# A fused recurrent-attention and feed-forward kernel on one core: its table of 2531 events in a new order

## The chip, the cores and the metric

The kernel runs on one core of a Trainium2 chip. The metric is device time in microseconds (us): the median over runs of the kernel, each run one execution of the whole program. The engines are TensorE (PE in the rows, with its weight loads as PEld), VectorE (DVE), ScalarE (ACT), GpSimd (POOL) and SyncE (SP), which here issues every DMA. Each engine executes its own instructions in the order in which they stand, and waits at semaphores for the others.

## The reference

For 32 heads (4 batches of 8), 768 steps and a head width of 48, a state matrix is carried from step to step and read before it is updated; then every token's 384 outputs go through a feed-forward layer with 2048 hidden units.

```python
k_n = k / (norm(k) + 1e-06)
for t in range(S):
    kt, vt, bt = (k_n[:, :, t], v[:, :, t], beta[:, :, t, None])
    y[:, :, t] = np.einsum('bhd,bhde->bhe', q[:, :, t], state)
    v_old = np.einsum('bhde,bhd->bhe', state, kt)
    state = state + bt[:, :, :, None] * np.einsum('bhd,bhe->bhde', kt, vt - v_old)
# x: y as (3072 tokens, 384)
h = x @ w_in
sp = np.maximum(h, 0.0) + np.log1p(np.exp(-np.abs(h)))
return (h * erf(sp)) @ w_out
```

## The kernel before

**The attention half** works on 12 chunks c of 64 steps. For each chunk the keys are loaded and squared (`load_step` L165, `norm_sq` L183 on ACT), summed and turned into step sizes (`norm_sum` L191 and `norm_ops` L202 to L215 on DVE), and their Gram matrices are made on PE (`gram_mm` L247 and L251) and scaled (`gram_d` L264, `gram_a` L258 on DVE). A triangular inverse follows. For chunks 0 and 1 it is done on DVE: `first_blocks` (L316, a transpose), 15 times `first_row` (L322 and L323), `first_back` (L327 and L329, two transposes), then small products on PE (`first_w` L340, `first_x` L351) with ACT and DVE copies of their results (`first_copy` L333, `first_w2` L344, `first_x2` L355). For later chunks POOL does it row by row (`solve_row` L363 and L364). Two halves are merged by `merge_t` (L391, DVE), `merge_e` (L400, PE), `merge_e2` (L405), `merge_z` (L413, PE), `merge_z2` (L417) and `merge_m` (L426, PE). Then 48 chain steps j, four per chunk, carry the state: `chain_u` (L461), `chain_s` (L474) and `chain_y` (L488) on PE, with DVE (`chain_u2` L467, `chain_s2` L482) or ACT between them.

**The feed-forward half** works on 12 groups g of 256 tokens. `x_tr` (L644, L645) transposes a group's outputs, two instructions per half; `x_all` (L523) spreads its maximum; `x_hi` (L661, ACT) and `x_lo` (L666, DVE) split it into two f16 parts. `ffn1` (L678) makes 16 blocks of the hidden layer, nine matmuls each; softplus (`e_sp` L704) and erf (`e_erf` L709) on ACT need different tables, and where the set changes, `table` puts an ACT_TABLE_LOAD in (L128). `h_out` (L691), `e_mul` (L713), `e_split` (L724, L722) and `e_rest` (L728) make two f16 parts of the product, and `ffn2` (L739 to L741), six matmuls per block, makes the output.

**The weights** arrive as 64-bit numbers and are made into f16 pairs in the kernel. `w_load` (L533) loads a twelfth of one matrix (512 KB); `w_mask` (L539, ACT), `w_low` (L543) and `w_bits` (L547, both DVE) rebuild a f32 from it. Four `w_sum` (L554, ACT) take the largest value of the matrix, `w_all` (L523, PE) spreads it, `w_scale` makes a scale of it, and for each of 16 blocks `w_hi`, `w_dif` (L603, L604: two f32 products and one f16 product on PE) and `w_lo` make the two parts. For `w_in` all this stands ahead of the first `ffn1`.

**The order.** Every call stands in a list of events with a due time. The list is sorted, and then a table of numbers, `ORDER`, puts it in the order in which the calls are made; that is the order of instructions on each engine. SP's queue is such an order too, and all loads and stores stand in it. 158 matmuls on a cleared tile (`warm`, `fill`, L143) compute nothing; they keep TensorE at work in the opening stretch.

```python
    ev.sort(key=lambda e: (e[0], e[1]))
    if ORDER:
        ev = [ev[i] for i in ORDER]
    ...
        for _, _, fn in ev:
            fn()
```

## Time and profile before

| what | before |
|---|---|
| median of 3 runs | 661.63 us (660.23 to 662.59) |
| the profiled execution's own time | 663.63 us |
| its span, first to last instruction | 661.9 us |
| granted TensorE clock, mean over the span | 0.986 |
| PE busy, PEld busy | 630.6 us (95%), 481.5 us (73%) |
| DVE, ACT, POOL busy | 468.8 us (71%), 468.6 us (71%), 357.7 us (54%) |

Busy time is the union of an engine's instructions. Matmuls are pipelined, so one that is given as 326 ns may stand 163 ns behind the one before it; distances between starts tell more of PE than durations. The profiled execution took 2.00 us more than the median.

### The profile page before, as it was taken

How to read it: one execution, taken by the hardware profiler on the slowest of the kernel's cores; microseconds unless marked ns; L12 is line 12 of the kernel's file. 1: busy time of each engine (PE TensorE's matmuls, PEld its weight loads, DVE VectorE, ACT ScalarE, POOL GpSimd, SP SyncE). 2: the span in 40 equal slices, each digit the busy share in tenths (PEclk: the TensorE clock that was granted, in tenths of full speed). 3: DMA queues.
4: the chain of work that ended last, by engine and by line, in shares of the span. 5: the costliest groups of instructions: out<-in, count | busy, mean ns of one | idle time of the engine just before them, and what ended most of it. 6: DMA issues, size and time to landing. Idle time of an engine off the chain costs nothing.

```text
span 661.9 us, 22889 instructions
## 1 busy us (share of the span) xinstructions
PE 630.6 (95%) x9866; PEld 481.5 (73%) x9866; DVE 468.8 (71%) x1032; ACT 468.6 (71%) x694; POOL 357.7 (54%) x524
## 2 busy tenths in 40 slices
PE   6788999999999999999899999999999999999996
PEld 4556668777768787777687677887776787777763
DVE  4977869878877886668766778875649765657541
ACT  2187898999768897656684677667566788768860
POOL 5081289779997259782489942239972321211322
PEclk8878999999999999999999999999999999999999
DMA  9875761673121740504622241531204210000102
GB/s 246 283 214 164 195 182 34 127 140 77 39 90 29 164 106 3 126 16 112 146 46 56 76 87 26 127 78 31 52 18 104 46 39 13 14 1 1 37 1 48
DMA packets 76421, 56.20 MB, mean 85 GB/s; under 512 B 57184, under 2 KB 66528, under 8 KB 76320
## 3 DMA queue, kind: packets, MB, share of 16 engines
q1 hardware_dynamic: 76320, 54.74, 33.9%
q8 instruction: 77, 1.26, 0.8%
q14 instruction: 24, 0.20, 0.1%
HBM read 42.14 MB, written 12.58 MB: 83 GB/s over the span
## 4 chain that ended last, share of the span: by engine, by line
PE 53%; DVE 16%; ACT 13%; POOL 7%; issue 5%; DMA 4%; SPq 1%; POOLq 0%; DVEq 0%; ACTq 0%
PE ph L678 17%; PE pr L739 7%; PE pr L741 6%; PE pr L740 6%; DVE H L713 3%; POOL xb L364 3%; ACT L128 3%; POOL tmp L363 2%; PE warm L143 2%; ACT L L709 2%; PE pc L488 2%; DVE H L691 2%; PE pm L426 1%; DVE z L467 1%; ACT L L704 1%
## 5 line engine op out<-in xcount | busy, mean ns | idle before, releaser
L678 PE MATMUL ph<-xh,w_in 128*128 128x256 f16 x1152 | 207.6, 273 | 2.7 <-ACT L L704 2.3
L678 PEld LDWEIGHTS <-w_in 128*128 128x128 f16 x1728 | 164.9, 98 | 30.2 <-issue 3.8
L128 ACT ACT_TABLE_LOAD x131 | 168.1, 1283 | 2.2
L728 POOL TENSOR_TENSOR L<-H,L 128x512 f16<-128x512 f32 x72 | 85.3, 1195 | 147.6 <-DVE L L724 96.7
L678 PE MATMUL ph<-xl,w_in 128*128 128x256 f16 x576 | 157.0, 273 | 0.0
L741 PE MATMUL pr<-w_out,L 128*128 128x384 f16 x384 | 125.2, 326 | 0.7 <-POOL L L728 0.7
L739 PE MATMUL pr<-w_out,L 128*128 128x384 f16 x384 | 125.4, 327 | 0.0
L740 PE MATMUL pr<-w_out,L 128*128 128x384 f16 x384 | 125.2, 326 | 0.0
L448 POOL TENSOR_TENSOR z<-v,nm 64x192 f32<-64x192 f32 x96 | 56.4, 587 | 104.6 <-DMA v<-vtok 59.8
L704 ACT ACTIVATE L<-ph,xct 128x512 f32<-128x512 f32 x96 | 65.7, 687 | 53.5 <-DVE H L691 48.5
L364 POOL TENSOR_TENSOR xb<-xb,tmp 128x31 f32<-128x31 f32 (+15 forms) x155 | 95.0, 613 | 12.2
L363 POOL TENSOR_TENSOR tmp<-gb,xb 128x31 f32<-128x31 f32 (+15 forms) x155 | 85.1, 549 | 27.0 <-DMA gb<-d 16.7
L713 DVE TENSOR_TENSOR H<-H,L 128x512 f32<-128x512 f32 x96 | 75.6, 795 | 27.9 <-ACT L L709 23.6
L691 DVE TENSOR_SCALAR H<-ph 128x512 f32<-128x512 f32 x72 | 49.2, 685 | 36.0 <-PE ph L678 27.5
L709 ACT ACTIVATE L<-L 128x512 f32<-128x512 f32 x96 | 58.6, 627 | 0.8
L741 PEld LDWEIGHTS <-L 128*128 128x128 f16 x384 | 37.6, 98 | 26.1 <-POOL L L728 1.4
L739 PEld LDWEIGHTS <-L 128*128 128x128 f16 x384 | 37.5, 98 | 21.8
L740 PEld LDWEIGHTS <-L 128*128 128x128 f16 x384 | 37.6, 98 | 20.8
L467 DVE TENSOR_TENSOR z<-pc,ga 64x192 f32<-64x192 f32 x80 | 28.4, 355 | 27.5 <-PE pc L461 26.0
L661 ACT ACTIVATE xh<-pt,xsx 64x128 f16<-64x128 f32 (+1 forms) x72 | 26.0, 395 | 24.6 <-PE pt L645 12.7
L143 PE MATMUL warm<-zero 128*128 128x384 f16 x158 | 35.0, 373 | 3.3 <-issue 2.2
L724 DVE CAST L<-H 128x512 f16<-128x512 f32 x72 | 35.7, 500 | 1.4
(157 smaller groups left out, 968.5 us busy)
## 6 DMA issues: line engine op xcount, KB each, us to landing
raw_in<-w_in SPq DMA_DIRECT2D x12, 512.0 KB, 8.0
raw_out<-w_out SPq DMA_DIRECT2D x12, 512.0 KB, 5.0
d<-A SPq DMA_DIRECT2D x20, 256.0 KB, 3.2
kpg<-kT SPq DMA_DIRECT2D x24, 192.0 KB, 4.5
k<-ktok SPq DMA_DIRECT2D x12, 384.0 KB, 4.6
v<-vtok SPq DMA_DIRECT2D x48, 96.0 KB, 2.7
qp<-qT SPq DMA_DIRECT2D x24, 192.0 KB, 3.5
out<-ob SPq DMA_DIRECT2D x48, 96.0 KB, 2.2
```

Of the source, the lines that this page charges most:

```text
L128: se.add_instruction(mybir.InstLoadActFuncSet(name=nc.get_next_instruction_name(), act_func_set_id=i, ins=[], outs=[]))
L363: ge.tensor_tensor(tv, G[:, s, s + 1:].unsqueeze(1).broadcast_to([P, ncol, nr]), Xv[:, :, s:s + 1].broadcast_to([P, ncol, nr]), op=ALU.mult)
L364: ge.tensor_tensor(Xv[:, :, s + 1:], Xv[:, :, s + 1:], tv, op=ALU.add)
L678: te.matmul(ph, w[:, i, kt * P:kt * P + P], G[x][:, :, ksl], start=(m == 0), stop=(m == 8))
L691: ve.tensor_scalar(dst, src, HSC, None, op0=ALU.mult)
L704: se.activation(unit("L", g, u), G["ph", u], AF.Softplus, bias=0.0, scale=G["ct"])
L709: se.activation(Lu, Lu, AF.Erf, bias=0.0, scale=1.0)
L713: ve.tensor_tensor(Hu, Hu, unit("L", g, u), op=ALU.mult)
L728: (ge if (g * NFF // EU + u) % GLM else ve).tensor_tensor(G["gl", u], unit("H", g, u), G["gh", u], op=ALU.subtract)
L739: te.matmul(G["po"][a], gh[:, o, asl], wout_h[:, i, :], start=(i == 0), stop=False)
L740: te.matmul(G["po"][a], gh[:, o, asl], wout_l[:, i, :], start=False, stop=False)
L741: te.matmul(G["po"][a], gl[:, o, asl], wout_h[:, i, :], start=False, stop=(i == NFF - 1))
```

## The change

`ORDER` is replaced by another permutation of the same 2531 events. All else in the file is the same.

```diff
-ORDER = (1,56,2,4,88,42,3,23,13,36,...)
+ORDER = (1,27,2,7,63,5,81,3,48,4,42,...)
```

Every engine executes the same instructions as before, with one exception: an ACT_TABLE_LOAD is made where softplus follows erf or erf softplus, and the new order has 139 such changes in place of 131. On PE the number of places where a f16 matmul is followed by a f32 one goes from 114 to 104.

**SP, the first loads.** `kpg` and `k` are the keys of a chunk in two layouts (the number behind the name is the chunk), `be` the step sizes, `raw_in` a twelfth of `w_in`, `v` values, `qp` queries. Before:

```order
L232 DMA kpg0_128<-kT 48x1024 x2
L165 DMA k0_133<-ktok 128x768
L533 DMA raw_in3_136<-w_in 128x1024
L165 DMA k1_139<-ktok 128x768
L232 DMA kpg1_141<-kT 48x1024 x2
L171 DMA be0_145<-btok 128x32
```

Now:

```order
L232 DMA kpg1_128<-kT 48x1024 x2
L165 DMA k1_132<-ktok 128x768
L165 DMA k0_135<-ktok 128x768
L232 DMA kpg0_138<-kT 48x1024 x2
L171 DMA be0_142<-btok 128x32
L533 DMA raw_in2_147<-w_in 128x1024
```

The load of a twelfth of `w_in` moved from between the two chunks' keys to behind them.

**DVE, the end of the first inverse.** L322 and L323 are its rows, L327 and L329 the transposes back. Before:

```order
L323 TENSOR_TENSOR w_out_101<-w_out_101 128x2x15
L543 TENSOR_SCALAR raw_in4_282<-raw_in4_282 128x512
L547 SCALAR_TENSOR_TENSOR w_in_100<-w_in_100,raw_in3_136 128x512
L327 STREAM_TRANSPOSE w_out_101<-w_out_101 128x32x32
L329 STREAM_TRANSPOSE w_out_101<-w_out_101 128x32x32
```

Now:

```order
L322 TENSOR_TENSOR w_out_101<-w_out_101 128x30
L323 TENSOR_TENSOR w_out_101<-w_out_101 128x2x15
L327 STREAM_TRANSPOSE w_out_101<-w_out_101 128x32x32
L543 TENSOR_SCALAR raw_in1_321<-raw_in1_321 128x512
L329 STREAM_TRANSPOSE w_out_101<-w_out_101 128x32x32
```

A `w_low` and a `w_bits` moved from ahead of the transposes to behind the first. Another such pair stood among the 15 rows and is gone from there, and one of the eight `gram_d` ahead of the first transpose (L316) now stands far behind it.

**ACT, the first instructions and those ahead of `first_w2` of chunk 0** (L344 on `pw0`). Before:

```order
L539 ACTIVATE w_in_100<-raw_in3_136 128x512
L183 ACTIVATE w_out_101<-k0_133 128x768
L183 ACTIVATE w_out_101<-k1_139 128x768
...
L344 COPY w_out_101<-pw1_508 128x256
L539 ACTIVATE w_in_100<-raw_in8_328 128x512
L333 COPY xm0_0_90<-w_out_101 32x16x32
L344 COPY w_out_101<-pw0_601 128x256
```

Now:

```order
L183 ACTIVATE w_out_101<-k1_132 128x768
L183 ACTIVATE w_out_101<-k0_135 128x768
...
L344 COPY w_out_101<-pw1_490 128x256
L273 COPY qp1_0_88<-pq1_0_361 64x512
L273 COPY qp1_1_89<-pq1_0_361 64x512
L539 ACTIVATE w_in_100<-raw_in3_182 128x512
L539 ACTIVATE w_in_100<-raw_in0_332 128x512
L539 ACTIVATE w_in_100<-raw_in2_147 128x512
L333 COPY xm1_1_93<-w_out_101 32x16x32
L344 COPY w_out_101<-pw0_584 128x256
```

The squares no longer stand behind a `w_mask`; between the two copies of `pw` there are now six instructions where there were two.

## Rows read from the trace of the kernel before

**Rows 1.** The page, busy time of each engine, its share of the span and instructions.

```profile
PE 630.6 (95%) x9866; PEld 481.5 (73%) x9866; DVE 468.8 (71%) x1032; ACT 468.6 (71%) x694; POOL 357.7 (54%) x524
```

**Rows 2.** Busy time by stretch: the stretch, its length, busy us and instructions of PE, PEld, DVE, ACT and POOL, the granted TensorE clock, DMA share and GB/s.

```profile
0.00:80.00 80.00, 65.37 (x1539) 43.88 (x1540) 59.60 (x149) 43.17 (x72) 29.75 (x42) 0.89 0.77 222
80.00:200.00 120.00, 117.68 (x1876) 90.61 (x1871) 95.83 (x209) 103.19 (x176) 100.37 (x146) 1.00 0.43 99
200.00:656.00 456.00, 447.26 (x6469) 347.03 (x6465) 312.80 (x674) 321.77 (x448) 227.57 (x337) 1.00 0.25 57
```

**Rows 3.** Groups of instructions by line, the matmuls that compute nothing: count, busy us, mean ns, idle time before them and what ended it.

```profile
L143 PE MATMUL warm<-zero 128*128 128x384 f16 x158 | 35.0, 373 | 3.3 <-issue 2.2 <-DVE zero L134 1.1
```

**Rows 4.** Who waited for whom on PE from 80 to 660 us: us in total, times, longest. There are 14 rows, which come to 9.7 us together; the first, one between and the last stand here.

```profile
PE ph L678 <- ACT L L704: 2.3, 4, 0.8
...
PE pc L488 <- DVE z L467: 0.5, 1, 0.5
...
PE pc L474 <- DVE z L467: 0.2, 1, 0.2
```

**Rows 5.** ACT in order of time from the start: start us, duration us, line, in square brackets the idle time ahead and what ended it.

```profile
7.92 0.66 ACT L539 ACTIVATE w_in<-raw_in 128x512 f32<-128x512 f32 x1 [5.90 <-DMA raw_in<-w_in]
8.48 0.83 ACT L183 ACTIVATE w_out<-k 128x768 f32<-128x768 f32 x1
9.63 0.84 ACT L183 ACTIVATE w_out<-k 128x768 f32<-128x768 f32 x1 [0.32 <-DMA k<-ktok]
```

**Rows 6.** The chain of work that ended last, 10 to 34 us, in order of time: start us, us, what.

```profile
10.63 0.87 DVE n L191
...
15.67 2.66 DVE w_out L264 x8
...
22.62 0.34 DVE raw_in L543
...
24.73 0.60 DVE w_in L547
...
29.90 0.32 DVE raw_in L543
30.22 0.60 DVE w_in L547
30.82 1.86 DVE w_out L327
...
32.81 1.25 PE pw L340 x82
```

**Rows 7.** The same chain, 36 to 75 us. "issue" is time in which PE waited for nothing that the profile shows.

```profile
36.14 2.44 issue
...
40.13 2.99 PE warm L143 x9
...
49.41 2.15 issue
51.56 3.66 PE warm L143 x13
...
57.22 0.58 ACT T L405
...
70.88 0.46 PE spin L523 x2
...
74.28 0.84 PE wd_in L603 x2
```

**Rows 8.** ACT in order of time, one row for each kind of instruction that the new order puts between 30 and 60 us: start us, duration us of the row, line, count.

```profile
26.73 1.19 ACT L273 COPY qp<-pq 64x512 f32<-64x512 f32 x2 [12.59 <-PE pq L251]
...
32.90 0.67 ACT L539 ACTIVATE w_in<-raw_in 128x512 f32<-128x512 f32 x1
...
42.54 0.60 ACT L333 COPY xm<-w_out 32x512 f32<-32x512 f32 x1
...
47.34 0.36 ACT L355 COPY xm<-pw 16x256 f32<-16x256 f32 x1
...
64.62 1.47 ACT L554 ACTIVATE raw_in<-w_in 128x1536 bf16<-128x1536 f32 x1
```

**Rows 9.** PE in order of time around 210 us, two f16 matmuls and the f32 product behind them: start us, duration us, line, count.

```profile
209.92 0.27 PE L678 MATMUL ph<-xl,w_in 128*128 128x256 f16 x1
210.03 0.27 PE L678 MATMUL ph<-xh,w_in 128*128 128x256 f16 x1
210.23 1.15 PE L251 MATMUL pg<-kpg 48*64 48x64 f32 x32
```

**Rows 10.** ACT and DVE in order of time from 128 us, the split of half a group's outputs: start us, duration us, line, count.

```profile
128.07 1.08 ACT L661 ACTIVATE xh<-pt,xsx 128x256 f16<-128x256 f32 x3
...
129.42 1.09 DVE L666 SCALAR_TENSOR_TENSOR xl<-pt,xsx,xh 128x256 f16<-128x256 f32 x3
```

**Rows 11.** Groups of instructions by line, the table loads: count, busy us, mean ns, idle time before them.

```profile
L128 ACT ACT_TABLE_LOAD x131 | 168.1, 1283 | 2.2
```

**Rows 12.** Busy time by stretch as in Rows 2, for 300 to 400 us.

```profile
300.00:350.00 50.00, 47.34 (x835) 38.00 (x833) 37.08 (x85) 34.59 (x49) 24.82 (x39) 1.00 0.44 101
350.00:400.00 50.00, 47.81 (x661) 36.15 (x658) 38.23 (x77) 31.71 (x45) 36.67 (x56) 1.00 0.31 72
```

More of the change, by code (lines that the diff above doesn't have):

```diff
@@ new lines @@
+ORDER = (1,27,2,7,63,5,81,3,48,4,42,6,450,12,65,13,32,49,9,77,58,37,43,52,66,14,68,64,73,57,44,78,360,82,11,85,8,98,105,102,101,10,93,108,19,17,202,89,254,109,183,18,208,238,118,146,121,228,124,15,128,23,132,24,135,25,26,139,28,29,142,30,31,147,33,34,151,35,38,154,39,40,158,41,45,46,47,163,188,50,51,53,166,153,162,170,231,54,184,59,60,61,62,67,70,71,270,75,76,88,91,229,288,177,36,20,56,79,241,80,284,84,191,86,185,87,90,92,227,95,96,273,130,99,161,205,243,21,74,249,114,221,55,100,212,104,106,94,107,251,299,110,112,194,219,305,149,449,312,72,22,223,215,451,198,206,113,16,115,210,116,117,120,122,256,123,125,217,127,313,129,131,134,247,197,316,200,456,234,322,235,199,136,137,140,169,144,141,97,143,145,148,126,150,152,297,464,155,138,156,159,160,164,260,165,472,168,236,172,173,176,174,245,175,179,171,180,181,182,237,186,187,280,189,192,267,252,459,222,445,193,1051,265,195,196,232,325,327,203,261,204,293,207,471,264,209,211,303,213,285,214,216,218,167,220,225,178,271,467,262,157,226,278,230,233,103,440,239,279,240,242,306,244,544,224,246,248,307,643,263,292,275,318,287,323,111,69,250,253,83,255,258,259,266,486,465,391,257,119,296,343,447,310,455,483,133,460,336,311,268,344,269,272,274,276,277,350,328,281,507,282,283,329,286,330,356,190,315,403,347,366,491,319,405,331,337,289,201,290,334,487,291,294,340,529,439,526,489,346,422,503,342,502,560,348,441,362,295,433,298,355,300,301,302,353,452,442,304,308,523,448,309,314,461,317,357,444,454,320,324,359,326,364,332,477,335,497,367,511,361,338,546,370,446,474,375,321,458,368,468,492,469,373,384,478,363,374,555,341,475,377,488,380,509,563,339,345,382,351,369,354,358,352,371,476,548,376,381,385,463,393,510,470,383,473,372,349,390,479,395,365,388,392,379,576,386,484,400,416,396,670,408,480,333,490,398,389,397,694,387,411,482,641,413,498,399,429,519,401,394,653,559,402,378,696,505,419,495,406,599,493,404,501,407,424,513,514,409,410,428,521,436,412,494,508,415,438,527,516,512,417,414,534,679,531,481,420,418,683,538,466,542,443,485,500,496,545,453,525,684,499,518,462,547,552,504,522,687,457,421,537,557,533,528,425,532,536,540,515,688,551,423,562,657,691,638,584,564,517,568,426,695,567,530,427,698,550,549,637,570,700,652,702,572,556,682,659,579,665,430,1049,541,721,585,553,664,654,431,535,588,646,561,587,714,590,741,520,432,434,697,598,565,616,524,701,577,606,722,435,596,703,613,554,578,593,506,724,731,569,621,597,437,769,748,539,573,603,625,711,566,580,737,582,629,604,543,574,558,571,586,755,632,575,623,581,639,644,611,602,583,601,592,666,607,594,628,612,677,610,655,615,743,589,752,618,620,681,732,758,600,624,635,765,622,689,671,633,848,650,645,707,720,685,706,728,626,883,649,692,746,730,693,595,690,712,757,709,723,717,719,745,605,784,627,713,735,1750,608,715,762,811,756,669,796,609,800,772,699,614,716,662,822,705,734,619,833,744,630,803,739,759,754,631,750,718,747,634,766,777,749,636,763,738,674,768,640,771,807,774,789,795,642,773,764,775,781,776,778,686,786,647,785,736,648,790,767,792,818,708,793,1069,710,783,651,805,798,799,656,865,797,831,658,726,804,829,660,873,661,813,801,837,810,832,812,663,780,742,842,845,948,725,782,877,704,913,787,727,897,729,838,1083,753,733,740,836,846,667,751,889,824,850,760,814,834,854,668,924,808,890,816,841,843,788,672,901,673,835,851,675,770,676,819,856,904,678,817,866,826,802,860,827,867,825,859,809,779,869,864,870,680,791,934,806,868,862,884,617,1073,815,847,794,878,839,905,844,876,849,852,1054,840,1089,853,882,914,830,857,855,886,875,828,861,858,872,879,917,863,871,921,885,874,922,918,880,898,887,881,908,892,888,896,972,946,895,900,1161,932,961,902,891,983,910,964,1064,894,920,820,953,931,911,899,956,927,903,906,985,909,916,761,959,937,923,943,997,929,993,1074,954,907,988,941,990,912,976,945,1077,968,915,984,1005,925,989,1078,919,970,1019,928,1081,926,1008,939,971,935,1014,952,1007,940,947,1047,955,950,1202,893,957,1053,962,930,933,1013,1037,1082,996,1021,958,1085,973,936,938,1087,1102,1086,1040,942,979,1084,1088,1031,951,960,1046,1110,1090,965,1092,1093,967,1095,978,1056,1131,1146,974,1097,1062,966,963,1059,1112,1132,821,949,1098,995,977,1018,1015,1028,1002,1068,969,980,1063,981,1138,1140,1034,1010,986,1071,944,1030,975,1066,1033,1311,982,1387,1035,1003,987,991,1039,994,1017,992,1042,1043,1122,1070,1048,1105,1120,1050,1121,1023,1113,1079,1124,1125,1139,1108,1020,1128,1107,1000,1029,1026,1136,1032,1094,1011,1142,1126,1012,1151,1228,999,1022,1221,1016,1080,998,1443,1027,1041,1100,1130,1096,1072,1111,1129,1103,1004,1001,1210,1076,1156,1382,1144,1145,1106,1178,1025,1044,1162,1232,1165,1038,1134,1239,1167,1147,1055,1172,1099,1101,1254,1057,1104,1149,1262,1058,1024,1247,1060,1150,1177,1241,1281,1157,1294,1422,1344,1179,1137,823,1159,1184,1160,1181,1045,1182,1250,1109,1168,1115,1197,1169,1257,1052,1175,1208,1176,1119,1061,1171,1153,1427,1217,1192,1135,1399,1276,1224,1188,1230,1258,1199,1200,1036,1148,1265,1234,1154,1185,1269,1267,1195,1240,1285,1183,1268,1190,1187,1067,1416,1244,1158,1320,1075,1201,1141,1206,1174,1114,1246,1118,1324,1272,1335,1273,1288,1327,1428,1209,1396,1248,1218,1164,1065,1198,1220,1297,1214,1203,1223,1091,1226,1252,1117,1227,1155,1204,1116,1225,1166,1291,1127,1173,1292,1123,1215,1133,1231,1259,1143,1211,1235,1194,1261,1152,1236,1264,1348,1287,1163,1242,1351,1293,1266,1205,1170,1243,1299,1270,1180,1189,1233,1186,1368,1275,1237,1309,1006,1278,1212,1207,1249,1339,1219,1316,1282,1216,1277,1289,1431,1346,1380,1432,1229,1298,1347,1315,1303,1352,1302,1295,1238,1318,1222,1325,1433,1245,1424,1283,1213,1435,1359,1274,1310,1256,1290,1314,1438,1436,1263,1280,1313,1524,1284,1271,1300,1286,1319,1371,1356,1251,1376,1384,1321,1379,1253,1381,1255,1363,1403,1373,1440,1451,1441,1437,1322,1406,1331,1329,1412,1418,1304,1360,1459,1308,1413,1388,1444,1353,1296,1455,1400,1307,1333,1420,1340,1334,1429,1336,1383,1326,1342,1496,1260,1393,1279,1497,1341,1395,1464,1462,1398,1330,1343,1454,2161,1306,1301,1332,1456,1401,1317,1305,1009,1323,1338,1473,1565,1405,1409,1350,1414,1312,1415,1328,1471,1354,1337,1365,1503,1370,1345,1355,1486,1458,1446,1469,1430,1193,1584,1408,1442,1453,1452,1196,1445,1450,1378,1488,1762,1507,1366,1474,1617,1489,1480,1374,1460,1625,1377,1375,1358,1349,1467,1514,1478,1492,1357,1466,1472,1477,1508,1386,1476,1461,1493,1407,1361,1541,1479,1463,1411,1485,1494,1501,1419,1490,1509,1505,1391,1520,1191,1392,1364,1394,1421,1484,1495,1423,1502,1522,1498,1523,1537,1519,1426,1385,1525,1531,1362,1512,1528,1534,1447,1511,1530,1546,1449,1545,1535,1434,1558,1468,1389,1465,1631,1517,1510,1470,1487,1555,1639,1390,1564,1540,1553,1513,1404,1475,1557,1542,1621,1547,1628,1570,1410,1560,1417,1640,1571,1569,1532,1580,1425,1538,1397,1539,1610,1515,1630,1657,1500,1636,1481,1550,1504,1806,1587,1518,1674,1561,1745,1660,1947,1562,1551,1439,1593,1683,1563,1596,1367,1604,1600,1597,1668,1572,1672,1603,1577,1613,1578,1612,1679,1607,1527,1448,1581,1521,1609,1483,1583,1457,1529,1536,1611,1482,1599,1615,1614,1568,1586,1591,1589,1698,1573,1616,1605,1759,1622,1491,1618,1606,1499,1624,1506,1627,1588,1632,1594,1787,1711,1516,1714,1629,1635,1526,1595,1633,1598,1602,1533,1567,1638,1543,1644,1682,1574,1734,1566,1685,1549,1654,1623,1696,1649,1641,1651,1655,1731,1620,1656,1646,1645,1544,1678,1369,1650,1652,1402,1637,1548,1785,1739,1662,1665,1661,1552,1659,1694,1666,1790,1663,1687,1673,1681,1579,1676,1658,1809,1719,1592,1653,1980,1791,1601,1576,1794,1684,1608,1690,1688,1619,1664,1707,1795,1781,1779,1796,1887,1693,1575,1722,1372,1582,1777,1697,1740,1692,1699,1626,1585,1689,1798,1703,1801,1783,1634,1792,1705,1744,1721,1706,1716,1695,1723,1643,1671,1763,1647,1746,1675,1712,1648,1701,1928,1709,1733,1717,1556,1748,1667,1704,1559,1756,1670,1827,1766,1758,1799,1849,1642,1677,1669,1761,1877,1702,1860,1834,1680,1710,1764,1715,1686,1718,1691,1765,1803,1836,1700,1729,1804,1743,1726,1817,1752,1768,1814,1769,1736,1793,1771,1737,1818,1800,1775,1747,1807,1816,1724,1708,2070,1727,1819,1822,1753,1772,1770,1757,1776,1713,1754,1778,1720,1773,1909,1821,1866,1826,1900,1824,2037,1782,1825,1920,1851,1728,1725,1738,1829,1742,1855,1933,1805,1870,1749,1784,1839,1810,1786,1856,1858,1812,1872,1788,1832,1808,1755,1835,1813,1865,1741,1823,1874,1868,1871,1861,1880,1815,1859,1881,1916,1890,1828,1892,1873,1882,1899,1894,1888,1875,1897,1751,1831,1876,1921,1833,1852,1878,1891,1994,1840,1893,1883,1554,1898,1837,1767,1885,1841,1931,591,1774,1843,1844,1886,1838,1842,1904,1903,1847,1780,1846,1930,1760,1789,1857,1864,1802,1905,1918,1848,1910,2003,1830,1811,1908,1923,1915,1820,1934,1884,1845,1926,1907,1973,1943,1911,1984,1853,1895,1950,1991,1956,1901,1902,1939,1967,1960,1732,1951,1927,1735,1935,1993,1932,1966,1797,1913,1976,1983,1970,1854,1924,1925,1590,1936,1914,1850,1940,1954,1944,1941,1946,1999,1972,1949,1862,1952,1869,2103,1958,1962,1988,1974,1995,2002,1968,1879,1998,1937,1978,1969,1889,1957,1896,1985,1961,1906,2013,2020,2000,1987,2014,1965,1863,1912,1990,2035,1867,1992,2007,2009,2042,2061,2072,2026,1929,2017,1959,1938,2074,1942,2082,2077,1996,2016,2019,1955,2025,1945,2023,2001,2065,2086,1948,2073,2078,1964,2004,2079,2008,2106,2041,2096,2015,1971,2024,2028,2029,2036,1982,2044,2039,2046,2051,2012,1989,2018,1997,2006,2021,2010,2085,2110,2047,1963,2005,2108,2045,2271,2151,2097,2048,2040,1977,1953,2059,2031,2162,1975,2057,1979,2094,1981,2060,2052,2294,2055,2062,2198,2056,2176,2022,2126,2027,2011,2221,2050,2120,2129,2030,2102,2066,2135,2058,2140,2068,2197,2145,2165,2084,2136,2107,2069,2087,2190,2032,2090,1730,2033,2123,2064,2169,1917,2075,2053,2043,2080,2092,2117,2081,2049,2034,1919,2038,2067,2054,1922,1986,2119,2105,2155,2063,2142,2148,2071,2113,2118,2122,2076,2124,2170,2083,2128,2132,0,2109,2131,2137,2111,2089,2138,2206,2166,2160,2164,2091,2217,2181,2178,2101,2099,2192,2104,2114,2219,2183,2115,2212,2172,2189,2220,2195,2334,2121,2100,2202,2226,2207,2236,2203,2242,2231,2223,2193,2232,2088,2216,2209,2130,2167,2225,2133,2215,2156,2228,2143,2224,2291,2158,2243,2116,2141,2229,2171,2144,2245,2146,2173,2196,2175,2248,2288,2253,2199,2258,2153,2180,2149,2201,2154,2095,2159,2208,2252,2240,2174,2177,2298,2250,2112,2204,2251,2302,2254,2187,2127,2303,2233,2300,2134,2179,2093,2257,2139,2185,2098,2188,2147,2235,2191,2307,2264,2152,2348,2274,2210,2269,2324,2260,2211,2255,2261,2265,2272,2292,2157,2297,2321,2277,2213,2266,2218,2182,2256,2230,2150,2262,2184,2168,2163,2263,2237,2268,2270,2280,2186,2286,2125,2273,2194,2275,2200,2312,2283,2304,2287,2205,2279,2289,2214,2317,2282,2222,2306,2227,2323,2259,2345,2247,2343,2313,2346,2351,2308,2336,2326,2318,2234,2328,2371,2366,2338,2239,2244,2361,2281,2342,2319,2284,2357,2325,2238,2293,2339,2241,2396,2359,2362,2340,2365,2383,2364,2295,2367,2393,2370,2347,2330,2375,2267,2381,2333,2349,2399,2309,2278,2374,2311,2285,2314,2315,2401,2403,2353,2290,2316,2320,2296,2377,2332,2422,2388,2378,2299,2327,2301,2390,2335,2412,2392,2322,2414,2305,2329,2415,2394,2417,2310,2382,2331,2395,2398,2408,2400,2337,2379,2419,2426,2404,2405,2384,2355,2409,2432,2385,2406,2352,2246,2341,2411,2421,2249,2356,2344,2424,2350,2369,2427,2354,2358,2360,2363,2441,2380,2368,2435,2372,2448,2443,2445,2425,2446,2276,2452,2449,2373,2451,2454,2429,2376,2485,2468,2387,2462,2475,2478,2386,2397,2389,2437,2391,2402,2439,2407,2487,2440,2455,2489,2410,2467,2423,2431,2505,2413,2479,2434,2416,2436,2420,2457,2418,2480,2458,2433,2430,2463,2438,2476,2442,2444,2477,2447,2502,2450,2459,2453,2428,2471,2461,2456,2464,2504,2460,2506,2490,2509,2465,2470,2469,2496,2473,2466,2472,2498,2510,2511,2492,2499,2474,2501,2482,2493,2481,2486,2513,2488,2516,2491,2518,2495,2483,2494,2507,2484,2497,2508,2519,2500,2512,2503,2514,2517,2515,2520,2521,2522,2523,2524,2525,2526,2529,2527,2528,2530)
```

1 line of the change is left out of this document (removed).

## The prediction

> **What bounds the kernel now.** I read the page first: PE is busy for 95% of the span and no other engine for more than 71% [rows 1]. Then busy time by stretch: the 95% hides two regimes [rows 2]. [...] Third, the waits on PE from 80 us on: 14 rows, 9.7 us together, none over 2.3 [rows 4]. So an order can gain little behind 80 us. What it can move is the point at which PE's useful work becomes dense.
>
> Last I read the chain ahead of that point. It runs through a load and ACT [rows 5], DVE from 10 to 32.8 us [rows 6], and then PE, with dummies and two stretches of "issue" in it, and ACT [rows 7]. It reaches the first block of `w_dif` at 74.28 us. I take that block as the milestone, since the new order puts exactly the same products ahead of it on PE, with 138 dummies ahead of it where there were 140. What comes behind it on PE is therefore the same work too, and if the milestone comes X earlier and nothing new is waited for behind it, the end comes X earlier.
>
> **Term 1, the first loads: -2.2 us.** Before, a `w_mask` stood first on ACT, so the first square started at 8.48 us, behind a weight load; the second waited for its key load until 9.63 [rows 5], and the sum behind it started at 10.63 [rows 6]. The weight load came in by 7.92 and the 384 KB of keys behind it by 9.63: 1.7 us. The 512 KB of weights at that rate take 2.3 us, so the first keys were there by about 5.6. Now the two key loads follow each other ahead of all weights: the second is there by about 7.4 (estimate from those three times), its square of 0.84 ends at 8.3, and the sum can start at 8.4, 2.2 us earlier. Bounds: 0, if the second load is as late as now, and -2.6, if it is there at 7.0.
>
> **Term 2, DVE's first inverse: -2.2 us.** Out of DVE's unbroken run between that sum and L327 go two `w_low` (0.34 + 0.32), two `w_bits` (0.60 + 0.60) and one of eight `gram_d` (2.66 / 8 = 0.33) [rows 6]: 2.2 us. They come back behind it, where ACT sets the pace (term 3). L327 then starts at 30.82 - 4.4 = 26.4.
>
> **Term 3, from the inverse to the milestone: -5.6 us more.** L327, a `w_low` and L329 end at about 26.4 + 1.86 + 0.32 + 1.9 = 30.5. `first_w` of chunk 1 takes 1.25 behind L327 [rows 6], so its copy ends at 29.9. Then ACT has six instructions: a pair L273 (1.19), three masks (0.67 each), one L333 (0.60) [rows 8], 3.8 us, and the other copy ends at 34.1. To the end of the second `merge_e2` of chunk 0 it then has 8 masks (5.4), 2 squares (1.7), 6 L333 (3.6), 3 L355 (1.1), a pair L273 (1.2) and the two L405 (1.2): 14.2 us, to 48.3. Before, that point was 57.22 + 0.58 = 57.8 [rows 7]. Why 9.5 us earlier and not 4.4: before, PE stood 2.44 us in "issue", and had 9 dummies for 2.99 us and 13 for 3.66 on the chain [rows 7]; now ACT's own work fills those stretches, and PE's dummies lie beside it. That goes on: `merge_z` (1.2 on PE), a pair L417 (1.2), 1.0 for the last copies, a table load (1.28) [rows 11], four `w_sum` (1.6 each) [rows 8], a mask and a pair L405 (1.9) come to 13.0, so 61.3; from `w_all` to `w_dif` it was 74.28 - 70.88 = 3.4 [rows 7], of which 0.6 is a `chain_u` that now stands earlier. That makes 64.1, or -10.2 us. I take **-10** for terms 1 to 3 together, because PE has little to spare there: between the two `merge_z` are 25 dummies and some 5.6 us of products in 9.7 us. [...] Bounds: -4.4 (only terms 1 and 2 survive) and -12.
>
> **Term 4, behind the milestone on PE: +1.** A f32 product behind a f16 matmul starts 0.20 us after it, another f16 one 0.11 [rows 9]. With 104 such places in place of 114 that gives -0.9. Against it stand tighter places. Counted in PE work by the order, at 9 x 0.11 = 0.98 us per `ffn1` block, four groups now have 1.90, 2.08, 2.08 and 2.45 us between their last `x_tr` and the first `ffn1` that reads it; before, none had under 2.52. The split between takes 1.08 on ACT and then 1.09 on DVE, of which three parts overlap a little [rows 10]; with 2.5 as the need the shortfalls come to 1.5. And a `chain_y` stands only 1.0 us behind its `chain_u` six times, where it was three; the one such wait in the trace took 0.5 [rows 4]. Together about +2, so +1 net. Bounds: -1 and +6, if every tight place waits twice its shortfall.
>
> **Term 5, ACT's table loads: 0.** Eight more, at 1283 ns each [rows 11], are 10.3 us of ACT. They lie around the fourth and fifth group (11 more there, 2 fewer in the first), where ACT idles 100 - 66.3 = 33.7 us of 100 [rows 12]. That idle time hides them; if it were gone, they would cost 10.3. The rows show 2.2 us of idle time ahead of all 131 together [rows 11]. [...]
>
> **Term 6, the other waits behind the milestone: 0**, since they were 9.7 us [rows 4] and the new ones can't be read from the order. Bounds: -6 and +8.
>
> Sum: 663.63 - 10 + 1 = 654.6 for an execution like the profiled one, which took 2.0 us more than the median. So **652.6** for the median.
>
> **The rivals.**
> - *The opening gains as said, and the waits shrink too* (0.22). For it: between a `chain_u` and its `chain_s` the new order has a median of 5.2 us of PE work, before 4.5. Against: 9.7 us [rows 4] is all there is. With -12 and -6: 663.6 - 12 - 6 - 2 = 643.6.
> [...]
> - *The head start is eaten* (0.08): ACT is busy for 103.19 of 120 us between 80 and 200 [rows 2] and sets the pace there, so PE arrives early and waits. Against it: ACT's work ahead of that stretch is no more than before, and it idled 36.8 of the first 80 us [rows 2]. 663.6 + 1 - 2 = 662.6.
> - *Slower, by the table loads* (0.08). The place is the fourth and fifth group: 11 more loads are 14.1 us of ACT, and L704 must read one of two `ph` buffers before PE can fill it again. L704 already heads PE's waits [rows 4]. If the loads bunch where a buffer is due, up to 14.1 us reach PE: 652.6 + 14.1 = 666.7. It decides from the point where over 11 of the 14.1 us land on PE; 33.7 idle us speak against that. [...]
>
> **How the numbers follow.** A measurement of this kernel can tell 0.3%, 2 us, from no change: faster means under 659.6, slower over 663.6. My forecast has 0.47. Its own range is 648 to 657. Faster: 0.47 + 0.22 + 0.12 of the third case = 0.81. Same: the rest of the third, 0.03, and 0.06 of the head start eaten = 0.09. Slower: the rest, 0.10. From 641 to 662 the range leaves out a third of the first rival and the slower cases, some 2 in 10.
>
> **What would show it.** Right: the second L191 starts near 8.4 us, L327 near 26, the second L405 of chunk 0 ends near 48, the first `w_dif` starts near 64, and from there to PE's last matmul it takes as long as before, within 3 us. ACT_TABLE_LOAD stands at x139 with PE's waits on L704 no longer than now. Wrong: the milestone comes after 70, with "issue" or dummies at 0.33 us on the chain ahead of it; or it comes early and PE's waits from there on come to over 15 us; or the fourth and fifth group take longer than before.

## The result, and the profile after

The new order is slower: 667.26 us (median of 20 runs, 663.86 to 672.47) against 662.89 us of the order before (20 runs on the same chip), a ratio of 1.0065 with a 95% interval of 1.0044 to 1.0086. The prediction was 652.6 us and faster. The profiled execution of the new order took 672.47 us, the longest of the 20, so below I lean on medians and on what several traces share, not on the length of one.

The page and the stretches, which answer to [rows 1, 2, 11]:

```profile
span 670.7 us, 22870 instructions
PE 636.6 (95%) x9866; PEld 486.3 (73%) x9866; DVE 473.4 (71%) x1032; ACT 480.3 (72%) x702; POOL 357.2 (53%) x524
L128 ACT ACT_TABLE_LOAD x139 | 178.3, 1283 | 2.4
```

```profile
0.00:80.00 80.00, 68.57 (x1557) 47.50 (x1559) 61.64 (x148) 42.64 (x72) 28.94 (x42) 0.96 0.75 223
80.00:200.00 120.00, 116.53 (x1873) 90.34 (x1870) 98.59 (x212) 102.31 (x175) 100.89 (x146) 1.00 0.42 97
200.00:656.00 456.00, 441.93 (x6388) 342.92 (x6387) 311.72 (x672) 333.75 (x455) 225.49 (x336) 0.99 0.26 58
```

Behind 200 us PE now idles 456 - 441.93 = 14.1 us where it idled 8.7, and the granted clock is 0.99 in place of 1.00. The table loads are 139, as forecast.

**The opening.** DVE in order of time (start, duration, what), and the chain of work that ended last, 10 to 75 us (start, us, what), which answers to [rows 6, 7]:

```profile
9.00 0.95 DVE L191 TENSOR_REDUCE n<-w_out 128x16 f32<-128x768 f32 x1 [1.56 <-ACT w_out L183]
...
27.93 1.97 DVE L327 STREAM_TRANSPOSE w_out<-w_out 128x1024 f32<-128x1024 f32 x1
```

```profile
12.17 1.52 issue
...
21.91 6.26 PE warm L143 x21
...
34.38 2.39 issue
...
43.38 3.69 issue
...
48.09 6.27 PE warm L143 x28
54.36 1.13 PE pe L400 x64
...
73.70 0.84 PE wd_in L603 x2
```

The inverse is ready 2.8 us earlier, but from 10 us on the chain runs through PE alone: its products, its dummies (27.7 us of the chain) and "issue" (8.6 us). By its own row the first `w_dif` starts at 73.6 us; it was 74.2.

**Behind it.** PE's largest waits from 80 us on, which answer to [rows 4] (who for whom: us, times, longest):

```profile
PE sp L523 <- DVE xm L624: 2.8, 4, 1.0
PE ph L678 <- ACT L L704: 2.1, 4, 0.9
PE pm L426 <- DVE xl L666: 2.1, 1, 2.1
PE pr L741 <- POOL L L728: 1.8, 3, 1.1
PE pz L413 <- ACT T L405: 1.5, 1, 1.5
PE pc L474 <- DVE z L467: 1.4, 2, 1.1
```

PE in order of time around 228 us (in brackets the idle time ahead and what ended it):

```profile
227.74 1.20 PE L413 MATMUL pz<-xm,T 32*32 32x32 f32 x64 [1.50 <-ACT T L405]
229.93 0.79 PE L523 MATMUL sp<-ident,xm 128*128 128x128 f32 x2 [0.99 <-DVE xm L624]
230.52 0.53 PE L739 MATMUL pr<-w_out,L 128*128 128x384 f16 x1
230.84 0.53 PE L740 MATMUL pr<-w_out,L 128*128 128x384 f16 x1
...
235.82 0.33 PE L741 MATMUL pr<-w_out,L 128*128 128x384 f16 x1
235.98 0.27 PE L644 MATMUL pt<-ident,y 128*128 128x128 f32 x1
```

Behind two waits of 1.5 and 0.99 us, 15 matmuls stand 0.32 us apart in place of 0.16, at a granted clock of 0.50 from 231 to 235.5 us: 2.4 us more. The waits themselves start on other queues. The first starts on DVE. L413 needs both halves of a copy L405; ACT's half waited 3.42 us for DVE's, and that stood behind an `e_mul` (L713) of 1.77 us:

```profile
223.99 1.77 DVE L713 TENSOR_TENSOR H<-H,L 128x512 f32<-128x512 f32 x1
...
226.39 0.68 DVE L405 COPY T<-pe 32x512 f32<-32x512 f32 x1
```

The median of the 96 L713 is 0.68 us; this one ran beside POOL's L728 (224.06 to 225.21), of which the last section has more. Eight traces have the new rest without a mending at this place. In seven the L713 there took 1.77 to 2.00 us and L413 waited 1.5 to 1.7 us; in the eighth (`after_half_dummies`) no L713 there was over 1.2, and L413 did not wait over 1 us.

The second wait starts on SP. SP, then DVE, in order of time:

```profile
218.40 0.46 SPq L369 DMA_DIRECT2D d<-xb  x1
221.36 1.92 SPq L384 DMA_DIRECT2D xm<-d  x4
223.38 2.52 SPq L289 DMA_DIRECT2D d<-A  x2
```

```profile
228.40 0.69 DVE L258 TENSOR_TENSOR A<-pg,gn 128x512 f32<-128x512 f32 x1 [1.33 <-DMA d<-A]
```

`to_dram` (L289) stands on SP behind `from_blocks2` (L384) of chunk 5, which waits for the store of `put_blocks` (L369) and is not needed before 248 us. So the store of A is late, `gram_a` (L258) waits to overwrite A, and all that is behind it on DVE, the maximum L624 among it, waits too; PE's 0.99 us are for L624.

A second such place is at 520 us. DVE and SP in order of time, then two `ffn1` pairs from the chain, 512 to 546 us:

```profile
523.85 0.62 DVE L747 TENSOR_SCALAR ob<-pr,xco 128x384 f32<-128x384 f32 x1 [2.99 <-DMA out<-ob]
```

```profile
520.61 0.35 SPq L441 DMA_DIRECT2D v<-vtok  x1
521.05 4.55 SPq L755 DMA_DIRECT2D out<-ob  x6
```

```profile
532.31 3.63 PE ph L678 x18
...
537.12 2.08 PE ph L678 x18
```

A store of output stands on SP behind loads of `v` that wait for POOL; DVE needs its buffer and waits 2.99 us; PE waits 0.84 us for L624 and 2.1 for L666 behind it, and then 18 matmuls take 3.63 us instead of 2.08, at a granted clock of 0.50 from 532.7 to 535.9 us (1.00 from 536.1 to 540). A third place, at 410 us, costs PE 2.2 us (waits for L728 on POOL and L704 on ACT).

### The profile page after: what moved, and what is told of

It reads as the page before. It is cut to its first block, busy times and chain, and to the rows that moved or that the text cites. A ratio compares the mean times of both kernels' runs of the same rounds, so it can differ in the third digit from the quotient of the medians.

```text
span 670.7 us, 22870 instructions
## 1 busy us (share of the span) xinstructions
PE 636.6 (95%) x9866; PEld 486.3 (73%) x9866; DVE 473.4 (71%) x1032; ACT 480.3 (72%) x702; POOL 357.2 (53%) x524
## 3 DMA queue, kind: packets, MB, share of 16 engines
q8 instruction: 77, 1.26, 0.8%
## 4 chain that ended last, share of the span: by engine, by line
PE 53%; DVE 16%; ACT 10%; POOL 10%; issue 5%; DMA 5%; SPq 1%; POOLq 0%; DVEq 0%; ACTq 0%
PE ph L678 15%; PE pr L739 6%; PE pr L741 6%; PE pr L740 6%; PE warm L143 4%; POOL xb L364 4%; POOL tmp L363 3%; ACT L128 3%; DVE H L713 2%; PE pc L488 2%; POOL L L728 2%; PE pc L461 2%; PE pq L251 2%; DVE H L691 2%; DMA d<-A 2%
## 5 line engine op out<-in xcount | busy, mean ns | idle before, releaser
L728 POOL TENSOR_TENSOR L<-H,L 128x512 f16<-128x512 f32 x72 | 85.4, 1197 | 163.7 <-DVE L L724 123.9
L704 ACT ACTIVATE L<-ph,xct 128x512 f32<-128x512 f32 x96 | 65.5, 687 | 56.4 <-DVE H L691 50.3
L448 POOL TENSOR_TENSOR z<-v,nm 64x192 f32<-64x192 f32 x96 | 53.6, 558 | 92.9 <-DMA v<-vtok 59.0
L363 POOL TENSOR_TENSOR tmp<-gb,xb 128x31 f32<-128x31 f32 (+15 forms) x155 | 87.5, 565 | 24.4 <-DMA gb<-d 14.4
L713 DVE TENSOR_TENSOR H<-H,L 128x512 f32<-128x512 f32 x96 | 73.5, 774 | 27.5 <-ACT L L709 14.6
L724 DVE CAST L<-H 128x512 f16<-128x512 f32 x72 | 41.0, 577 | 1.3
L666 DVE SCALAR_TENSOR_TENSOR xl<-pt,xsx,xh 64x128 f16<-64x128 f32 (+1 forms) x72 | 25.8, 386 | 15.5 <-ACT xh L661 15.0
```

Of the source, the lines that this page charges most:

```text
L363: ge.tensor_tensor(tv, G[:, s, s + 1:].unsqueeze(1).broadcast_to([P, ncol, nr]), Xv[:, :, s:s + 1].broadcast_to([P, ncol, nr]), op=ALU.mult)
L704: se.activation(unit("L", g, u), G["ph", u], AF.Softplus, bias=0.0, scale=G["ct"])
L713: ve.tensor_tensor(Hu, Hu, unit("L", g, u), op=ALU.mult)
L728: (ge if (g * NFF // EU + u) % GLM else ve).tensor_tensor(G["gl", u], unit("H", g, u), G["gh", u], op=ALU.subtract)
```

## The experiments

Medians of all kernels that were timed more than once (6 to 20 runs), with the ratio to the order before, measured beside it on the same chip. Where I compare two of these kernels with each other and their intervals overlap, the difference is not clear of noise.

| kernel | us | ratio, 95% interval |
|---|---|---|
| the new order | 667.26 | 1.0065, 1.0044 to 1.0086 |
| open_before_rest_after | 678.16 | 1.0231, 1.0206 to 1.0255 |
| open_after_rest_before | 664.86 | 1.0033, 1.0006 to 1.0059 |
| seam_before_after | 672.07 | 1.0130, 1.0082 to 1.0178 |
| seam_after_before | 661.05 | 0.9964, 0.9940 to 0.9989 |
| after_half_dummies | 664.65 | 1.0028, 1.0004 to 1.0052 |
| after_no_dummies | 665.90 | 1.0051, 1.0028 to 1.0075 |
| before_half_dummies | 664.87 | 1.0029, 1.0005 to 1.0054 |
| repair_220 | 670.75 | 1.0110, 1.0069 to 1.0151 |
| repair_220b | 665.38 | 1.0030, 1.0007 to 1.0052 |
| repair_520 | 664.42 | 1.0016, 0.9994 to 1.0038 |
| repair_all | 666.05 | 1.0048, 1.0023 to 1.0073 |
| repair_all_half | 667.47 | 1.0052, 1.0021 to 1.0082 |
| repair_three | 662.82 | 0.9994, 0.9970 to 1.0017 |

**Half of one order, half of the other, cut at the first `w_dif`.** The edit, in both directions:

```diff
-ORDER = new
+ORDER = p + [i for i in other if i not in p]   # p: one order up to w_dif("in", 0)
```

> All events up to the first w_dif of w_in stand as in the order before, all later ones as in the new order. Theory (the loss stands behind the opening: waits of DVE and PE in the new order from 200 us on, and TensorE's clock that falls behind two of them; the opening itself came out even): the first w_dif starts at 74.3 us as before, the time is some 668 us, ratio to before 1.005 to 1.010, and PE loses 5 to 10 us between 200 and 560 us as in the new order's profile. Rival A (the new opening hands on late work, and that is what costs later): with the old opening the later part loses nothing, 663 us, ratio 0.998 to 1.002.

> The reverse: the new order up to the first w_dif of w_in, the order before from there on. Theory (the loss stands behind the opening): the first w_dif starts at 73.6 us, and from there it takes as long as before: 662 us, ratio 0.997 to 1.001. Rival A (the new opening hands on late work): ratio 1.004 to 1.009, about 667 us.

Neither came out as expected by either theory. The cut itself cost time: from the first `w_dif` to the first `ffn2` it took 59.4 us (old opening, new rest) and 61.5 us (the reverse) where the two whole orders take 54.5 and 54.1. PE there waited 4.1 and 3.4 us for L611 on ACT; 15 events of the old opening and 9 of the new one stand on the other side of the cut in the other order. But the loss behind 200 us was there with the old opening as well. That called for a better cut.

**The same at a seam** where both orders have made the same events but for four (event 555, some 110 us):

> The new order for its first 555 events (to about 110 us), the order before for the rest; at that point the two have done the same events but for four. Theory (the opening gained some 3 us: six executions with the new opening whole reached the first ffn2 at 122.4 to 127.7 us, mean 125.3, the one of before at 128.7; the rest loses some 8): the gain stays and the loss is gone, 658 to 661 us, ratio 0.993 to 0.998. Rival A (the opening is worth nothing in the end): 662 to 664 us. Rival B (the seam costs what it did at the first w_dif): 664 us or more.

> The reverse: the order before for its first 555 events, the new order for the rest. Theory: the loss of the rest without the gain of the opening, 668 to 672 us, ratio 1.008 to 1.014, with PE idle for 3, 2 and 3 us in 200 to 240, 400 to 440 and 520 to 560. Rival A (the new opening hands on late work to the rest): 662 to 664 us.

The theory holds in both, each median less than 0.1 us beyond its range: the new opening with the old rest takes 661.05 us and beats both orders; the reverse takes 672.07. The opening's gain is smaller with the old rest (1.5 us by the medians) than with the new one (672.07 - 667.26 = 4.8). PE in three stretches (length, then busy us of PE, PEld, DVE, ACT, POOL, clock, DMA), the first kernel and then the second:

```profile
200.00:240.00 40.00, 39.91 (x710) 33.42 (x706) 35.53 (x85) 34.39 (x45) 18.27 (x32) 1.00 0.55 121
400.00:440.00 40.00, 39.37 (x661) 31.68 (x657) 30.49 (x73) 28.55 (x41) 7.67 (x13) 1.00 0.40 87
520.00:560.00 40.00, 39.69 (x612) 31.74 (x613) 23.96 (x51) 34.99 (x46) 7.32 (x9) 1.00 0.09 22
```

```profile
200.00:240.00 40.00, 36.99 (x603) 29.24 (x602) 32.95 (x72) 31.21 (x43) 22.12 (x35) 0.96 0.39 77
400.00:440.00 40.00, 37.90 (x536) 28.54 (x535) 30.66 (x73) 27.28 (x40) 11.05 (x15) 1.00 0.42 97
520.00:560.00 40.00, 37.34 (x694) 29.94 (x689) 26.71 (x61) 25.50 (x37) 6.41 (x8) 0.96 0.15 35
```

In the four traces with the old rest PE idles at most 0.8 us in each of these and the clock is 1.00 in all. In the thirteen with the new rest, mended or not, it idles up to 5.8 us in one, and in each of them the clock is below 1.00 in one to three of the three stretches. Where it falls differs from run to run (in 200 to 240 us from 0.91 to 1.00).

**Fewer dummies.**

```diff
-ORDER = new
+ORDER = [i for i in new if i not in dropped]   # dropped: every second, or all 130, fill() ahead of w_dif("in", 0)
```

> The new order with every second of the 130 dummies ahead of the first w_dif left out (they compute nothing). Theory (PE's dummies set the pace of the new opening: PE waits for no engine between 13.7 and 70 us, and 130 dummies take some 30 us there): 65 dummies less are up to 14 us less on PE, until ACT's chain sets the pace near 64 us; the first w_dif starts at 64 to 68 us and the time falls by 5 to 9 us against the new order, to 658 to 662 us, ratio to before 0.993 to 0.999. Rival C (PE's instructions can't come faster, so that the dummies only fill time that would stand in 'issue'): the first w_dif starts at 72 us or later, 'issue' on the chain grows from 8.6 us to over 15, and the time stays at 667 us.

> The new order with all 130 dummies ahead of the first w_dif left out. Theory (PE's dummies set the pace of the new opening): PE waits for ACT and DVE again; the first w_dif starts near 64 us, as worked out in the prediction for the chain of ACT. [...] Rival C (PE's instructions can't come faster): first w_dif at 72 us or later, with over 20 us of 'issue' ahead of it, and 667 us or more.

> The order before with every second of its 140 dummies ahead of the first w_dif left out (66 less). If PE's dummies hold up that opening too (in its chain 9 took 2.99 and 13 took 3.66 us), the first w_dif comes at 70 to 72 us in place of 74.3, and the time falls by 2 to 4 us, to 659 to 661, ratio 0.994 to 0.998. If ACT and DVE set the pace there, or the stretch behind it (80 to 200 us, where ACT is busy for 86%) takes the gain, the time is the same within 1 us.

The new order gained 2.6 and 1.4 us (its interval overlaps with both), the order before lost 1.8 (ratio 1.0029). With half, the first `w_dif` came at 72.0 us, with none at 69.7; not at 64, and within the 68.2 to 73.8 that eight traces with all dummies span. PE without dummies, in order of time:

```profile
45.43 0.56 PE L351 MATMUL pw<-w_out 32*16 32x16 f32 x44 [4.09 <-issue]
49.02 0.31 PE L400 MATMUL pe<-T,w_out 32*32 32x32 f32 x2 [3.03 <-DVE T L391]
49.76 1.91 PE L400 MATMUL pe<-T,w_out 32*32 32x32 f32 x62 [0.42 <-DVE T L391]
53.20 1.91 PE L413 MATMUL pz<-xm,T 32*32 32x32 f32 x64 [1.53 <-ACT T L405]
```

The products take 1.91 us a row instead of 1.20, at a granted clock of 0.50 between 30 and 60 us (0.89 in the new order), and "issue" comes to 8.4 us as before. So the dummies aren't simply in the way: with them such a row of products took 0.71 us less. The chain of this trace runs on DVE from 43 us to the first `w_dif`, 10 us of it `w_low` and `w_bits`. My theory that the dummies set the pace falls in that form, and so does rival C, which had over 15 and over 20 us of "issue".

In the opening the granted clock of a row doesn't tell all: from 22 to 27 us of the new order it is 1.00, yet the dummies there stand 0.32 us apart, as the matmuls do at 0.50 behind 231 us.

**DVE's weight work.**

```diff
-ORDER = new without the 130 dummies
+ORDER = the same without w_low("in", i) and w_bits("in", i)
```

> The new order without the 130 opening dummies, and with w_low and w_bits of w_in left out (24 instructions on DVE, some 12 us; the low parts of the weights are then missing). Theory D (with the dummies gone, DVE sets the pace between 43 and 69 us, through w_low and w_bits, which the prediction's chain of ACT did not count): the first w_dif comes at 63 to 66 us, where it came at 69.7 with them. Rival (ACT's own chain is that long): 68 us or later.

The kernel ran once (668.55 us). The first `w_dif` came at 71.3 us; theory D falls. The chain now ran through "issue" of 3.5 and 5.2 us ahead of L351 and PE's products, and hardly through DVE.

**What "issue" is.** In the thirteen traces of the new opening, whole or without dummies, I counted the matmuls ahead of each such stretch. They are always some of the same numbers, with or without dummies in between: 223, 349, 604, 732, 860, 988, 1115 and 1243, and in three traces a last one at 1369 or 1497. From 349 to 1243 these are 127, 128 or 255 apart. A matmul goes with a weight load (PE and PEld both have x9866), so 128 of them are 256 instructions. The page's queues (packets, MB, share):

```profile
q8 instruction: 77, 1.26, 0.8%
```

77 packets make 1.26 MB, 16.4 KB each; PE and PEld have 2 x 9866 = 19,732 instructions, 256 for each packet. I take it from these counts, as an estimate, that PE's instructions arrive in blocks of 256, and that "issue" is PE waiting for the next. The packets in the traces agree: of the 83 such stretches ahead of 75 us in all 17 traces, 82 end 1.2 to 1.7 us after one of these packets has landed. From 80 us on PE shows no such stretch in any trace; in the new opening they come to 5.5 to 11 us in twelve of its thirteen traces (the thirteenth comes next).

> The new order with each load of a twelfth of w_in cut to its first half, which is then read twice (w_low runs twice on half); ACT's and DVE's work stays the same within 0.1 us per piece, the weights are wrong. Theory F (PE's 'issue' stretches come at block boundaries of its instruction stream, and are long because the instruction blocks arrive late behind the loads): 'issue' ahead of 75 us falls from 8.6 us (5.5 to 11 in the other executions of this opening) to under 3. Rival G (a block takes its time whatever else is loaded, and PE runs through 128 tiny matmuls faster than that): 'issue' stays at 5 us or more.

The edit to the load, shortened (`w_mask`, `w_low` and `w_bits` then read the half twice):

```diff
-q.dma_start(raw, src[:, 2 * RW * i:2 * RW * (i + 1)])
+q.dma_start(raw[:, :RW // 2, :], src[:, 2 * RW * i:2 * RW * i + RW])   # w_in; read twice
```

PE's waits for "issue" ahead of 75 us were

```profile
PE warm L143 <- issue: 0.4, 1, 0.4
PE pw L351 <- issue: 0.2, 1, 0.2
```

0.6 us, so theory F holds in this one trace. The time did not follow: 676.79 us, once, and the first `w_dif` at 79.2 us. One thing is mixed in: DVE's rows L322 and L323 took up to 1.3 us in place of 0.3, beside instructions of POOL, and PE stood 7.9 us ahead of L340. But without dummies it stood 8.0 us there too, and "issue" still came to 8.4.

The packets of the profiled new order decide between F and G without that mixture. For four blocks (times in us): when PE began the block before, when the packet ran, and how busy the DMA engines were from the one to the other.

| block behind matmul | PE begins the one before | packet | DMA busy | "issue" |
|---|---|---|---|---|
| 604 | 31.36 | 34.40 to 35.37 | 0.88 | 2.39 |
| 732 | 36.77 | 37.91 to 38.87 | 0.05 | none |
| 860 | 40.06 | 44.65 to 45.64 | 0.98 | 3.69 |
| 988 | 47.08 | 48.12 to 49.19 | 0.01 | none |

Each packet took 1.0 to 1.1 us; it started 1.0 to 1.1 us behind PE's step where the DMA engines were idle, and 3.0 and 4.6 us behind it where the loads filled them. With the lighter loads the packet for 860 started 1.4 us behind it, though PE took the same 3.2 us for the block before. So in this trace the blocks come late behind the loads, as F has it.

**Mending single places of the new order.**

```diff
 repair_220: put_blocks(5), from_blocks2(5): -ahead of to_dram(6)  +behind to_blocks(6); ffn2(29), ffn2(30): +ahead of merge_z(4)
 repair_220b: the same, put_blocks(5) stays
 repair_520: ffn_store(5, 0): -behind load_v(44), load_v(41), load_v(43)  +ahead of put_blocks(11)
 repair_all: repair_220 + repair_520, e_rest(5, 3) +ahead of put_v(32), norm_ops(5, 2..3) +behind e_split(5, 4)
 repair_all_half: repair_all without every second of the 130 dummies
 repair_three: repair_220b + repair_520, e_rest(5, 3) and (5, 6) +ahead of their put_v, norm_ops(5, 2..3) +ahead of norm_ops(5, 4)
```

> The new order with one place mended: put_blocks and from_blocks2 of chunk 5 stand behind to_dram and to_blocks of chunk 6 on SP (as in the order before), and two ffn2 blocks stand ahead of the merge_z of chunk 4 on PE. Theory (the loss stands in three places at which PE waits for DVE or ACT): PE's idle time from 200 to 240 us falls from 3.3 us to under 1 us, the clock stays at 1.00 there, and the time falls by 2 to 4 us against the new order's 667.3, to 663 to 665 us, ratio to before 1.001 to 1.004. Rival B (the loss is spread over many small waits and dearer table loads, and the places only show where they add up): PE's waits turn up again behind that place, and the time stays within 1 us of 667.

> The new order with one store moved: ffn_store of the first half of group 5 stands ahead of put_blocks of chunk 11 on SP in place of behind three more loads. Theory (three places): DVE's 3.0 us wait at L747 for that store is gone, with it PE's waits of 0.84 us on L624 and 2.07 us on L666 and the fall of the clock behind them; time 663 to 665 us, ratio 1.001 to 1.004. Rival B (many small waits): within 1 us of 667.

> The new order with all three places mended: as above at 220 and 520 us, and at 410 us two sets of norm_ops (L207 to L209) behind the h_out and e_mul that PE and ACT wait for on DVE, and one e_rest ahead of a put_v that waits for its load on POOL. Theory (three places): PE idles from 200 to 560 us no longer than before (some 9 us), PE's time from the first ffn2 to the last falls from 536 us to 528 to 530, and the time to 658 to 661 us, ratio 0.993 to 0.998, faster than before. Rival B (many small waits): 665 to 668 us.

> The three places mended and every second of the 130 opening dummies left out. If the two losses are independent, the 2.6 us that half the dummies gave add to those of the mended places: 656 to 659 us, ratio 0.990 to 0.995. If a shorter opening only lets TensorE's clock fall later or PE arrive early where ACT sets the pace (80 to 200 us), it adds nothing: the same time as with the three places mended alone.

> As repair_220, but put_blocks of chunk 5 stays where the new order has it, and only from_blocks2 moves. In repair_220 POOL's solve_init (L303) waited for the moved put_blocks, and PE 3.7 us for the e_rest (L728) behind it. Theory (PE pays for single places where a queue is blocked by an event that is not due): without that new wait PE idles under 1.5 us from 200 to 240 us (3.3 in the new order), and the time is 663 to 666 us. Rival B (many small waits): 666 to 668 us.

> All three places mended again, with what the first repairs showed: only from_blocks2 moved at 220 us; at 410 us two e_rest ahead of the put_v they stand behind, and the two norm_ops behind merge_z2 and the sums of the group, just ahead of the next norm_ops; the store at 520 us as before. Theory (single places): the gains add up, PE idles under 10 us from 200 to 560 us and under 2 us in each of the three stretches 200 to 240, 400 to 440 and 520 to 560; 659 to 663 us, ratio 0.994 to 1.000. Rival B (many small waits): 664 us or more.

`repair_220` made it worse by 3.5 us (the intervals overlap): I had left `solve_init` on POOL where it was. POOL, then PE, in order of time:

```profile
225.34 0.95 POOL L303 MEMSET xb<- 128x1024 f32 x1 [12.02 <-DMA d<-xb]
```

```profile
228.83 0.34 PE L741 MATMUL pr<-w_out,L 128*128 128x384 f16 x1 [3.68 <-POOL L L728]
```

The moved `put_blocks` reads xb, L303 clears it and waited, and the `e_rest` behind it on POOL kept PE 3.68 us: the wait had changed its queue. `repair_all` carries the same fault and shows little: 666.05 us, in rival B's range. `repair_all_half` took 1.4 us longer still by the medians (0.3 by the ratios), so leaving out half the dummies, which was worth 2.6 us in the new order, was worth nothing here. `repair_520` took 2.8 us off, with one store moved; the stretch answers, with 1.57 us idle for 3.05 and the clock at 1.00:

```profile
520.00:560.00 40.00, 38.43 (x719) 31.27 (x717) 29.60 (x66) 28.30 (x40) 8.95 (x11) 1.00 0.13 30
```

`repair_220b` took 1.9 us off (the intervals overlap), but not as expected: with the two `ffn2` blocks ahead of it L413 waits no more, yet PE still idled 3.0 us in 200 to 240, now 2.2 of them for the copy L417 on ACT. Its trace has the clock at 1.00 there, the new order's 0.91; whether that is the gain, one trace can't say. `repair_three` took off 4.4 us, which is all of the net loss (0.9994, 0.9970 to 1.0017), some 0.3 less than the two alone add up to; its idle time in 400 to 440 is still 2.2 us, so the third mending did nothing that shows. On PE it did only a part of what was expected: 11.3 us idle from 200 to 560 us (14.1 in the new order), not under 10, and over 2 us in two of the three stretches. So small waits stay a rival for the rest of the loss.

## Why the prediction was wrong

**Terms 1 and 2** were right in kind: the second L191 started at 9.00 us (10.55 before, 8.4 forecast), L327 at 27.93 (30.74 before, 26.4 forecast). 2.8 us came of 4.4; the run between the two shrank by 1.3 instead of 2.2, two of the last rows of the inverse, beside POOL's L448, taking 0.47 and 0.53 us where they took 0.2.

**Term 3 failed, at "PE's dummies lie beside it".** The prediction let ACT set the pace to 64 us. ACT did not: it waited 5.2 us for `pw` and 4.3 us for `pe`, while PE waited for no engine between 13.7 us and the first `w_dif`. The prediction had counted the dummies on PE but taken "issue" as a thing of the old opening [rows 7], a stretch that ACT's work would fill; it is PE waiting for its instructions, 8.6 us of it, two of whose packets started 3.0 and 4.6 us behind PE's step while the loads ran, and its places go with the number of matmuls, which the new order hardly changed. Over eight executions of the new opening with all its dummies the first `w_dif` came at 68.2 to 73.8 us, mean 71.0; over three of the old one at 74.2 to 76.3, mean 75.2: a gain of 4.2 us, not 10, and in the profiled pair 0.6. That is the lower bound of 4.4 (only terms 1 and 2 survive), the third of the cases that the chances count (663.6 - 4.4 + 1 - 2 = 658.2 us): dummies 0.32 us apart (22 to 27 us) and "issue" stood on the path again. Why not earlier than 68 us is shown only in part: without the dummies DVE's weight work came onto the chain, without that work "issue" did, so several paths lie within a few us of each other, and no run took all of them away.

**Terms 4 and 6 failed in size.** They had +1 net and bounds of -6 and +8 for waits that "can't be read from the order". From the start of the first `ffn2` to the start of the last it took 524.7 to 528.5 us in four traces with the old rest (mean 526.8) and 531.7 to 536.7 in five with the new rest unmended (mean 534.8): +8.0. With -4.2 for the opening that makes +3.8; measured were +4.4. The 4.2 is rough: the medians at the seam gave 1.5 and 4.8. PE's idle time from 80 to 640 us went from 11.1 to 17.5 us, and behind two of the waits, at a granted clock of 0.50, the matmuls took 2.4 and 1.6 us more in the profiled run. The tight places that term 4 counted (shortfalls of 1.5 us) were not those that cost. The costly ones came from other queues, which the counting of PE's work between producer and consumer doesn't see: at 520 us from a store behind loads on SP (one moved store, 2.8 us), at 228 us from a DVE instruction beside POOL's and from a store on SP behind a transfer that wasn't due. In `repair_three` the stretch from the first `ffn2` to the last still took 530.3 us, 3.5 more than the old rest's mean. And no term had the clock behind 80 us in it.

Term 4's own count was off as well: `w_dif` ends with a f16 product, and with it the places where a f32 matmul follows a f16 one go from 124 to 116 in all (not 114 to 104), behind the milestone from 108 to 103; that is -0.5 us, not -0.9.

**Term 5 was right.** Eight more table loads cost nothing that shows: PE waited 2.1 us for L704 (2.3 before), and between 280 and 400 us, where the added loads lie, it idled 1.6 us for 5.6 before. The last rival had the right sign, and with 666.7 us nearly the measured time, by the wrong mechanism: that is luck. The idle time ahead of all 139 loads together is 2.4 us.

**What stays open:** how much of `repair_220b`'s gain is the clock, where the 3.5 us go that the rest still loses in `repair_three`, and which of the paths into the first `w_dif` would give way at what cost.

## What to carry to other kernels

When an order is made anew, read each in-order queue for an event that waits and isn't due, the DMA queue first: a store or load behind it can stop a compute engine two steps on (at 520 us DVE for 2.99 us, PE for 0.84 and 2.1 behind it), and a count of work between producer and consumer won't show it. A wait on PE can cost more than its length: behind the waits at 228 and 531 us of the new order the granted clock was 0.50, and the matmuls took 2.4 and 1.6 us more. And before an opening is credited with an engine's slack, ask whether PE's own instructions arrive in time: here "issue" was 8.6 us of the chain.
